# Adding the inverse transform's results by accumulating DMAs, with the second angle table built from sixteen direct slots

## The chip, the cores and the metric

The kernel runs on one core of a Trainium2 chip. The metric is the device time of one execution in microseconds, taken as the median of the runs shown. The engines are named as in the profile: PE (TensorE), ACT (ScalarE), DVE (VectorE), POOL (GpSimd) and SP (SyncE, which here only issues DMAs).

## The reference, cut to what matters

The input `x` has 2048 rows of 512 channels in bfloat16. The output is a gated mix of two branches:

```python
x = A_u                                            # (1, 2048, 512)
g = sigmoid((x * gate_w).sum(-1, keepdims=True))
a = _A_ref(x, ...)                                 # a long convolution per channel
b = _B_ref(x, ...)                                 # x plus a small FFN on the two rows that a router picks
return g * a + (1 - g) * b
```

Branch A convolves each channel `d` with a kernel of 2048 taps, which is a sum over 128 complex states, and adds a skip term:

```python
dt = exp(log_dt)[:, None]
logdA = dt * (A_re + 1j * A_im)                    # (512, 128)
P = exp(logdA[:, :, None] * l[None, None, :])      # l = 0..2047, rounded to bfloat16
K = einsum("dn,dnl,dn->dl", C, P, dt * B).real     # (512, 2048)
y = irfft(rfft(u, 2L) * rfft(K, 2L))[:L] + u * Dskip
```

## The kernel before

**What it computes in which order.** The 512 channels are worked in two halves of 256 (`h`, 0 and 1); the 2048 rows in two blocks of 1024 (`blk`). The stages are:

- `exps1` and `exps2` (L534 to L542): ACT computes magnitudes exp(t * dt * A_re) for both halves at once. `exps2` writes one copy for half 0 (`EB[0]`) and one to a staging place (`ST`), which a DMA parks in DRAM (L876) and another reads back for half 1 (L892).
- `routing` (L613): transposes, gate and router values, the FFN of the two picked rows.
- `tab1(h)` (L562): the first angle table, 32 slots of 256 values per part; `trig` (L543) supplies sines and cosines in groups of up to four slots: angle multiplies (L408), a Sin on ACT, a quarter-turn shift on DVE (L557), a second Sin.
- `tab2(h)` (L587): the second angle table `TQ[h]`, 21 slots of 256 values, real and imaginary, multiplied by the weights `w` (`WW`). Nine slots are computed directly and multiplied by `w` in one complex product; twelve more follow by two complex products of the first ones with two base factors (`BN`). `cmul` (L572) is one complex product of six DVE instructions.
- `forward` (L713): the transform of the input by matmuls (L731, L733).
- `xupd` (L864): `U` becomes (1 - g) times branch B's output.
- `kgen(h)` (L743): multiplies the two tables on PE into the kernel's taps by lag (L751), evacuates them to `KA[h]`, and regroups them by selection matmuls (L765 to L771) into `KC[h]`.
- `kspec(h)` (L775): the taps' spectrum by matmuls with the constant `KP` (L787).
- `products(h, qd, blks)` (L793): spectrum times spectrum on DVE, in quarters.
- `inverse(h)` (L826): matmuls back to rows (L841). For half 0, and for half 1's block 1, ACT writes g times the result to `YA` (L850), and a DVE addition of 128x1024 adds four rows of it to `U` (L854). For half 1's block 0 a DVE instruction does both from PSUM (L859). Then SP issues the stores, one for every two row tiles (L862).

**What sets the order.** Every operation is recorded with what it reads and writes (`Prog.op`); places in SBUF overlap, and a place can only be written when its last readers are done. `Prog.schedule` (L107) then plans the order of each engine by estimated costs: the operation that can start earliest goes first, and among equals the one with the longest estimated path to the end plus its priority:

```python
key = (st, -o.bl - o.prio)
```

Operations with a `tset` go by phases: all of phase 0 (the exponentials) is placed before any of phase 1 (Sin, Tanh, Silu). The engines run their queues strictly in the planned order. `EV` and `SCL` may go to ACT or DVE, as the planner finds earlier.

**Places that matter here.** `TQ[0]`, `ST`, `EB[1]` and `KA[1]` share one region; `TQ[1]`, `EB[0]` and `KA[0]` another. So the parked magnitudes can only be read back when `kgen(0)` has read all of `TQ[0]`, and `tab2(1)` can only write `TQ[1]` when half 0's selection has read `KA[0]`. `KP` lies where `TP[0]` was. `YA` has two parts by `t2`, which each block of rows reuses.

Of the kernel before, what the change touches and what calls it, by code (L numbers as in the profile page):

```python
# [9 lines left out]
BF = mybir.dt.bfloat16  # L10
# [48 lines left out]
class Prog:  # L59
# [47 lines left out]
    def schedule(self):  # L107
# [15 lines left out]
        dma_free = {SP: 0.0, ACT: 0.0}  # L123
# [135 lines left out]
T2 = [0, 1, 2, 3, 258, 256, 512, 768, 4, 5, 6, 7, 262, 260, 516, 772, 1024, 1280, 1536, 1792, 2048]  # L259
T2BASE = [(0, 4), (13, 17), (8,)]  # L260
NJ = len(T2)
ANG2 = [124 + t for t in T2[:8]] + [1148, 1024, 4]
MAG2 = [None] + T2[1:8] + [1024, 4]
NM = len(MAG2)
# [64 lines left out]
def bass_gated_mix__ssm_conv_s4__moe_arch_mod__prompt_kernel(nc, A_u, A_A_re, A_A_im, A_B_re, A_B_im, A_C_re, A_C_im, A_log_dt, A_Dskip,  # L329
# [24 lines left out]
    with ExitStack() as es:  # L354
# [85 lines left out]
        EB = [B("eb%d" % i, o, NM * 512) for i, o in enumerate((oG, oE))]  # L440
        ST = B("st", oE, NM * 512)
        PK = Buf(P, "park", AR[:, :], "dram", 0, 4, BF)
        park = nc.dram_tensor("park", (128, NM * 256), BF).ap()
        QA = [B("qa%d" % i, o + NM * 512, 9 * KB) for i, o in enumerate((oG, oE))]
        BN = [(B("bni%d" % i, o + 14 * KB, KB), B("bnr%d" % i, o + 15 * KB, KB)) for i, o in enumerate((oG, oE))]
# [91 lines left out]
        def exps2(ts):  # L537
            for b in (EB[0], ST):
                P.op(POOL, lambda h, b=b: h.memset(b(0, 128, 0, (4 * NM, 64), (1, 4)), 1.0), [], [(b, ("e", 0))], cost=0.4)
            for i, m in enumerate(MAG2):  # L540
                if i:
                    AC(two(EB[0], ST, i * 4, 4 * NM), AL(0, 128, 0, (HC, 2), (4, 64), (1, 4)), ACTF.Exp, [AL], [(EB[0], ("e", i)), (ST, ("e", i))], scale=float(m), tset=ts)  # L542
        def trig(h, angs, ts, neg):  # L543
# [5 lines left out]
            na_ = len(angs)  # L549
            ks = [(a, i) for i in range(na_)]  # L550
            lo = bass.AP(ah.tensor, ah.offset, [[ah.ap[0][0], 128], [2 * HC, na_], [8, 64], [2, 4]])
            n = na_ * HC
            def so(k):
                return s(0, 128, k * n, (4, na_), (4 * na_, 64), (1, 4))
# [17 lines left out]
        def cmul(h, outs, a, b, rda, rdb, wr):  # L572
            t = QA[h]
            o3 = outs(0).ap[1:]
            def q(i):
                d, st = [], 1
                for s_, c_ in reversed(o3):
                    d.insert(0, (st, c_))
                    st *= c_
                return t(0, 128, i * 9 * HC, *d)  # L580
            TT(q(0), a(0), b(0), MUL, rda + rdb, [(t, 0)])
            TT(q(1), a(1), b(0), MUL, rda + rdb, [(t, 1)])
            TT(outs(1), a(1), b(1), MUL, rda + rdb, wr(1))
            TT(outs(0), a(0), b(1), MUL, rda + rdb, wr(0))
            TT(outs(1), outs(1), q(0), SUB, [(t, 0)], wr(1))
            TT(outs(0), outs(0), q(1), ADD, [(t, 1)], wr(0))
        def tab2(h, ts):  # L587
            (qi, qr), (bi, br), eb = TQ[h], BN[h], EB[h]
            tq = lambda p: (qi, qr)[p]
            TW = 4 * NJ  # L590
            for g in range(3):
                s = trig(h, ANG2[4 * g:4 * g + 4], ts[g // 2], False)
                nn = len(ANG2[4 * g:4 * g + 4])
                for b_, kk, o_s, sk in ((qi, "s", 0, "s"), (qr, "c", 2 * nn * HC, "c")):
                    if g < 2:
                        TT(b_(0, 128, 16 * g, (TW, 64), (1, 16)), eb(0, 128, 16 * g, (4 * NM, 64), (1, 16)), s(0, 128, o_s, (16, 64), (1, 16)), MUL,
                           [(eb, ("e", 4 * g + i)) for i in range(4)] + [(s, sk)], [(b_, ("a", g))])
                    else:
                        bb = bi if b_ is qi else br
                        TT(b_(0, 128, 32, (TW, 64), (1, 4)), eb(0, 128, 32, (4 * NM, 64), (1, 4)), s(0, 128, o_s, (12, 64), (1, 4)), MUL,  # L600
                           [(eb, ("e", 8)), (s, sk)], [(b_, ("a", 2))])
                        TT(bb(0, 128, 0, (8, 64), (1, 8)), eb(0, 128, 32, (4 * NM, 64), (1, 8)), s(0, 128, o_s + 4, (12, 64), (1, 8)), MUL,
                           [(eb, ("e", 8)), (eb, ("e", 9)), (s, sk)], [bb])
            ka = lambda p: [(tq(p), ("a", g)) for g in range(3)]
            ks = ka(0) + ka(1)
            sl = lambda p, j, c: tq(p)(0, 128, 4 * j, (TW, 64), (4, c), (1, 4))
            cmul(h, lambda p: sl(p, 0, 9), lambda p: sl(p, 0, 9), lambda p: WW(0, 128, (1 - p) * D + h * HC, (4, 64), (0, 9), (1, 4)), ks, [WW], ka)
            bn = lambda p, j, c: (bi, br)[p](0, 128, 4 * j, (8, 64), (0, c), (1, 4))
            cmul(h, lambda p: sl(p, 13, 8), lambda p: sl(p, 0, 8), lambda p: bn(p, 1, 8), ks, [bi, br], lambda p: [(tq(p), "n")])
            cmul(h, lambda p: sl(p, 9, 4), lambda p: sl(p, 5, 4), lambda p: bn(p, 0, 4), ks, [bi, br], lambda p: [(tq(p), "f")])  # L610
# [132 lines left out]
        def kgen(h):  # L743
# [12 lines left out]
            for bk in range(3):  # L756
                pb = misc()
                def sel(hh, bk=bk, pb=pb):
                    last = None
                    base = T2BASE[bk]  # L760
                    njg = len(base)
# [192 lines left out]
```

## Time and profile before

| what | value |
|---|---|
| median of 3 runs | 193.92 us (193.47 to 194.07) |
| the profiled execution's own time | 193.47 us |
| its span, first to last instruction | 191.7 us |
| PE busy | 160.6 us (84%), mean granted clock 0.972 |
| DVE busy | 163.5 us (85%), 240 instructions |
| ACT busy | 130.4 us (68%), 214 instructions |
| POOL busy | 3.9 us (2%), 9 instructions |
| moved by DMA | 22.39 MB, mean 117 GB/s |

The profile is of one execution. "Busy" is the time in which an engine had an instruction under way; the span has stages with different limits, so the shares say little by themselves. A line number names the line that recorded the operation, which is often a helper: L389 is every DVE instruction on two tensors, L400 and L404 are ACT's activations and evacuations, L408 the angle multiplies, L393 instructions with a constant.

### The profile page before, as it was taken

How to read it: one execution, taken by the hardware profiler on the slowest of the kernel's cores; microseconds unless marked ns; L12 is line 12 of the kernel's file. 1: busy time of each engine (PE TensorE's matmuls, PEld its weight loads, DVE VectorE, ACT ScalarE, POOL GpSimd, SP SyncE). 2: the span in 40 equal slices, each digit the busy share in tenths (PEclk: the TensorE clock that was granted, in tenths of full speed). 3: DMA queues.
4: the chain of work that ended last, by engine and by line, in shares of the span. 5: the costliest groups of instructions: out<-in, count | busy, mean ns of one | idle time of the engine just before them, and what ended most of it. 6: DMA issues, size and time to landing. Idle time of an engine off the chain costs nothing.

```text
span 191.7 us, 3562 instructions
## 1 busy us (share of the span) xinstructions
PE 160.6 (84%) x1490; PEld 105.7 (55%) x1490; DVE 163.5 (85%) x240; ACT 130.4 (68%) x214; POOL 3.9 (2%) x9
## 2 busy tenths in 40 slices
PE   0066499999999999999998798996899999659691
PEld 0065444666344444565563166785688888437580
DVE  0658745899999999996717999999999999999983
ACT  3679999999989995499959963697345562232400
POOL 8000000000000000000000000000000000000000
PEclk9999669999999999999999999999999999978999
DMA  5999999309401202200099200000920001012133
GB/s 94 257 289 359 294 404 405 100 9 329 104 14 45 55 4 51 55 3 0 15 364 419 108 2 3 0 3 0 359 84 0 3 0 55 3 55 65 45 109 109
DMA packets 22097, 22.39 MB, mean 117 GB/s; under 512 B 13121, under 2 KB 19394, under 8 KB 21698
## 3 DMA queue, kind: packets, MB, share of 16 engines
q1 hardware_dynamic: 20738, 21.84, 35.8%
q10 hardware_dynamic: 1344, 0.33, 1.5%
q8 instruction: 11, 0.18, 0.4%
q14 instruction: 4, 0.03, 0.0%
HBM read 18.63 MB, written 2.75 MB: 112 GB/s over the span
## 4 chain that ended last, share of the span: by engine, by line
PE 46%; DVE 40%; ACT 4%; DMA 4%; issue 2%; SPq 1%; DVEq 0%
DVE AR L389 38%; PE ps L731 30%; DMA AR<-in_A_u_dram 4%; PE ps L751 3%; PE ps L841 2%; ACT AR L400 2%; ACT AR L404 2%; PE ps L733 2%; PE ps L706 2%; DVE AR L396 2%; PE ps L765 2%; PE ps L620 1%; PE ps L695 1%; SPq L484 1%; PE ps L632 1%
## 5 line engine op out<-in xcount | busy, mean ns | idle before, releaser
L389 DVE TENSOR_TENSOR AR<-AR 128x1024 bf16<-128x1024 bf16 (+7 forms) x148 | 130.4, 939 | 11.4 <-DMA AR<-in_A_A_re_dram 6.2
L404 ACT ACTIVATE AR<-ps 128x1024 bf16<-128x1024 f32 (+5 forms) x58 | 45.2, 818 | 27.0 <-PE ps L787 14.5
L731 PE MATMUL ps<-AR 128*128 128x512 bf16 x256 | 60.5, 387 | 0.0
L400 ACT ACTIVATE AR<-AR 128x512 bf16<-128x512 f32 (+4 forms) x73 | 50.5, 757 | 3.4 <-DVE AR L389 2.2
L731 PEld LDWEIGHTS ps<-AR 128*128 128x128 bf16 x256 | 24.8, 99 | 28.9 <-issue 2.3
L841 PE MATMUL ps<-AR 128*128 128x256 bf16 x256 | 30.9, 281 | 6.0 <-DVE AR L389 4.4
L841 PEld LDWEIGHTS ps<-AR 128*128 128x128 bf16 x256 | 25.3, 101 | 11.1 <-DVE AR L389 5.8
L400 ACT ACTIVATE AR<-ps,AR 128x256 bf16<-128x256 f32 (+1 forms) x40 | 19.9, 566 | 15.6 <-PE ps L841 10.2
L787 PE MATMUL ps<-AR 128*128 128x256 bf16 x224 | 26.2, 273 | 2.5 <-ACT AR L404 2.5
L787 PEld LDWEIGHTS ps<-AR 128*128 128x128 bf16 x224 | 21.3, 98 | 7.2 <-ACT AR L404 4.6
L408 ACT ACTIVATE AR<-AR 128x256 int32<-128x256 f32 (+1 forms) x41 | 17.2, 488 | 0.0
L620 PE MATMUL ps<-AR 128*128 128x128 bf16 x64 | 6.7, 289 | 11.9 <-DMA AR<-in_A_u_dram 11.0
L393 DVE TENSOR_SCALAR AR<-AR 128x1024 int32<-128x1024 int32 (+5 forms) x22 | 11.5, 529 | 1.8 <-ACT AR L400 1.5
L620 PEld LDWEIGHTS ps<-AR 128*128 128x128 bf16 x64 | 5.7, 133 | 12.7 <-DMA AR<-in_A_u_dram 11.0
L751 PE MATMUL ps<-AR 128*128 128x84 bf16 x256 | 11.7, 200 | 1.1 <-ACT AR L404 1.1
L751 PEld LDWEIGHTS ps<-AR 128*128 128x128 bf16 x256 | 10.8, 97 | 3.1 <-ACT AR L404 1.5
L869 PE MATMUL ps<-AR 128*128 128x512 bf16 x16 | 6.2, 386 | 1.7 <-ACT AR L400 1.4
L404 DVE CAST AR<-ps 128x1024 bf16<-128x1024 f32 (+1 forms) x6 | 6.8, 1125 | 0.5 <-PE ps L733 0.5
L408 DVE TENSOR_SCALAR AR<-AR 128x256 int32<-128x256 f32 (+1 forms) x21 | 5.6, 306 | 1.6 <-ACT AR L400 1.5
L765 PE MATMUL ps<-AR 128*32 128x128 bf16 (+1 forms) x96 | 6.4, 383 | 0.5 <-ACT AR L404 0.5
L404 DVE COPY AR<-ps 128x1024 bf16<-128x1024 bf16 (+1 forms) x6 | 4.1, 688 | 3.0 <-PE ps L620 2.8
L733 PE MATMUL ps<-AR 128*128 128x512 bf16 x16 | 6.1, 379 | 0.0
(37 smaller groups left out, 57.6 us busy)
## 6 DMA issues: line engine op xcount, KB each, us to landing
AR<-c_ksp SPq DMA_DIRECT2D x1, 3584.0 KB, 14.4
AR<-in_A_u_dram SPq DMA_DIRECT2D x2, 1024.0 KB, 8.7
AR<-c_fwd SPq DMA_DIRECT2D x1, 2048.0 KB, 7.9
AR<-c_fwdn SPq DMA_DIRECT2D x8, 256.0 KB, 4.3
AR<-c_inv SPq DMA_DIRECT2D x1, 2048.0 KB, 9.0
out_dram<-AR SPq DMA_DIRECT2D x16, 128.0 KB, 2.2
AR<-in_B_w_gate_dram SPq DMA_DIRECT2D x1, 1792.0 KB, 11.2
AR<-in_B_w_up_dram SPq DMA_DIRECT2D x2, 896.0 KB, 11.7
```

Source lines behind the costliest of these rows:

```text
L389: return P.op(DVE, lambda h: h.tensor_tensor(out=o, in0=a, in1=b, op=op), rd, wr, cost=tt_cost(o, a, b), **k)
L393: return P.op(DVE, lambda h: h.tensor_scalar(out=o, in0=a, scalar1=s1, scalar2=None, op0=op0), rd, wr, cost=c, **k)
L400: return P.op(ACT, lambda h: h.activation(out=o, in_=a, func=func, scale=scale, bias=bias), rd, wr, cost=0.185 + nel(o) * 0.833e-3 + (0.09 ...
L404: return P.op((ACT, DVE), (lambda h: h.activation(out=o, in_=a, func=ACTF.Copy), lambda h: h.tensor_copy(o, a)), rd, wr, cost=(0.185 + n * ...
L408: return P.op((ACT, DVE), (lambda h: h.activation(out=o, in_=a, func=ACTF.Copy, scale=c), lambda h: h.tensor_scalar(out=o, in0=a, scalar1= ...
L620: last = h.transpose(bb(0, 128, db * 256 + t_ * 128, (1, 128)), U(0, 128, (2 * q + t_) * D + db * 128, (1, 128)), IDN(0, (1, 128)))
L731: last = h.matmul(o, w, U(0, 128, (blk * 8 + st * 2 + par) * D, (1, D)), start=(par + st == 0), stop=(par * 4 + st == 7 and blk == 0))
L733: last = h.matmul(o, CB(0, 128, 640 if part == 0 else 512, (1, 128)), X(0, 128, (1 - part) * 2048 + (pm * 4 + ft) * 256, (8192, 2), (1, 25 ...
L751: last = hh.matmul(pb(0, 128, (g - b0) * 84, (1, 84)), TP[h][1 - part](0, 128, g * 128, (1, 128)), TQ[h][1 - part](0, 128, g * 84, (1, 84) ...
L765: last = hh.matmul(pb(32 * g, 32, c4, (256, njg), (4, 64)), lw, KA[h](0, 128, c4 + 4 * (base[0] + g), (16, njg), (84, 64)), start=True, st ...
L787: last = hh.matmul(pb(0, 128, n * 256, (1, 256)), KP(0, 128, u * 2048 + tau * 128, (1, 128)), KC[h](0, 128, jg * 256, (1, 256)), start=(k ...
L841: last = hh.matmul(pb(0, 128, e * 256, (1, 256)), G(0, 128, ((par * 2 + part) * 4 + ft) * 512 + (2 * t2 + e) * 128, (1, 128)), X(0, 128, h ...
```

## The change

Two things change together.

**The second table.** The list of slots `T2` is reordered. Sixteen magnitudes and angles are computed directly per half (`MAG2`, `ANG2`): eight that become slots 0 to 7, and eight multiples of 256 that become factors (`BS`). `trig` always takes four slots, so `tab2` has four groups. Groups 0 and 1 are each multiplied by `w` by a complex product of 1024 values; four more complex products (`far`, 4, 2, 2 and 5 slots) make slots 8 to 20. `cmul` uses three scratch parts where it used two and writes into its outputs only sums and differences. The parked copy and its two DMAs grow from 655,360 to 1,048,576 bytes; the read back stands behind the load of `KP` and has no priority of its own. The two POOL memsets of the exponentials' first slot go; that slot is an exponential too.

**The additions.** The DVE additions into `U` in `inverse` become DMAs issued by POOL that read `YA` and accumulate into `U`, 262,144 bytes each.

```diff
@@ -120,7 +120,7 @@
...
-        dma_free = {SP: 0.0, ACT: 0.0}
+        dma_free = {SP: 0.0, ACT: 0.0, POOL: 0.0}
@@ -256,12 +256,10 @@
 BLK, NBLK, HF, HC = 1024, 2, 2, 256
 T1 = [8 * k for k in range(16)] + [8 * (31 - k) for k in range(16)]
 ANG1 = [124 - 8 * s for s in range(16)]
-T2 = [0, 1, 2, 3, 258, 256, 512, 768, 4, 5, 6, 7, 262, 260, 516, 772, 1024, 1280, 1536, 1792, 2048]
-T2BASE = [(0, 4), (13, 17), (8,)]
+T2 = list(range(8)) + [256, 258, 260, 262, 512, 516, 768, 772, 1024, 1280, 1536, 1792, 2048]
 NJ = len(T2)
-ANG2 = [124 + t for t in T2[:8]] + [1148, 1024, 4]
-MAG2 = [None] + T2[1:8] + [1024, 4]
-NM = len(MAG2)
+ANG2 = [124 + b for b in range(8)] + [256 * a for a in range(1, 9)]
+MAG2 = list(range(8)) + [256 * a for a in range(1, 9)]
 KUSE = [(0, 0), (0, 1), (0, 2), (0, 3), (0, 4), (1, 4), (1, 5)]
 
 
@@ -437,12 +435,13 @@
         XT = B("xt", oD, 16 * KB)
         WG = B("wg", oF, 14 * KB); WD = B("wd", oF, 14 * KB)
         WU = [B("wu%d" % i, oB + (8 + 16 * i) * KB, 7 * KB) for i in range(2)]
-        EB = [B("eb%d" % i, o, NM * 512) for i, o in enumerate((oG, oE))]
-        ST = B("st", oE, NM * 512)
+        BS = [(B("bsi%d" % i, o, 4 * KB), B("bsr%d" % i, o + 4 * KB, 4 * KB)) for i, o in enumerate((oG, oE))]
+        EB = [B("eb%d" % i, o, 4 * KB) for i, o in enumerate((oG, oE))]
+        ST = B("st", oE, 8 * KB)
+        B_st = [lambda p0, n, c, *d, k=k: ST(p0, n, c + 2 * KB * k, *d) for k in range(2)]
         PK = Buf(P, "park", AR[:, :], "dram", 0, 4, BF)
-        park = nc.dram_tensor("park", (128, NM * 256), BF).ap()
-        QA = [B("qa%d" % i, o + NM * 512, 9 * KB) for i, o in enumerate((oG, oE))]
-        BN = [(B("bni%d" % i, o + 14 * KB, KB), B("bnr%d" % i, o + 15 * KB, KB)) for i, o in enumerate((oG, oE))]
+        park = nc.dram_tensor("park", (128, 4 * KB), BF).ap()
+        QA = [B("qa0", oG + 8 * KB, 7680), B("qa1", oE + 8 * KB, 7680)]
         NG = [B("ng%d" % i, oG + 16 * KB + 2 * i * KB, 2 * KB) for i in range(2)]
         ARG = [B("arg%d" % i, oI + 4 * i * KB, 4 * KB, I32) for i in range(2)]
         ARH = [b.base.bitcast(I16) for b in ARG]
@@ -535,23 +534,21 @@
             for s in range(32):
                 AC(two(TP[0][1], TP[1][1], s * 4, 128), AL(0, 128, 0, (HC, 2), (4, 64), (1, 4)), ACTF.Exp, [AL], [(TP[0][1], ("e", s)), (TP[1][1], ("e", s))], scale=float(T1[s]), tset=ts)
         def exps2(ts):
-            for b in (EB[0], ST):
-                P.op(POOL, lambda h, b=b: h.memset(b(0, 128, 0, (4 * NM, 64), (1, 4)), 1.0), [], [(b, ("e", 0))], cost=0.4)
             for i, m in enumerate(MAG2):
-                if i:
-                    AC(two(EB[0], ST, i * 4, 4 * NM), AL(0, 128, 0, (HC, 2), (4, 64), (1, 4)), ACTF.Exp, [AL], [(EB[0], ("e", i)), (ST, ("e", i))], scale=float(m), tset=ts)
+                k = i // 8
+                d = (EB[0], BS[0][1])[k]
+                AC(two(d, B_st[k], (i % 8) * 4, 32), AL(0, 128, 0, (HC, 2), (4, 64), (1, 4)), ACTF.Exp, [AL], [(d, ("e", i % 8)), (ST, i)], scale=float(m), tset=ts)
...
-            na_ = len(angs)
-            ks = [(a, i) for i in range(na_)]
-            lo = bass.AP(ah.tensor, ah.offset, [[ah.ap[0][0], 128], [2 * HC, na_], [8, 64], [2, 4]])
-            n = na_ * HC
+            ks = [(a, i) for i in range(4)]
+            lo = bass.AP(ah.tensor, ah.offset, [[ah.ap[0][0], 128], [2 * HC, 4], [8, 64], [2, 4]])
+            n = 4 * HC
             def so(k):
-                return s(0, 128, k * n, (4, na_), (4 * na_, 64), (1, 4))
+                return s(0, 128, k * n, (4, 4), (16, 64), (1, 4))
@@ -569,7 +566,8 @@
...
-        def cmul(h, outs, a, b, rda, rdb, wr):
+        def cmul(h, outs, a, b, nd, rda, rdb, wr):
+
             t = QA[h]
@@ -577,37 +575,44 @@
...
-                return t(0, 128, i * 9 * HC, *d)
...
+            TT(q(0), a(1), b(1), MUL, rda + rdb, [(t, 0)])
+            TT(q(1), a(0), b(0), MUL, rda + rdb, [(t, 1)])
+            TT(q(2), a(1), b(0), MUL, rda + rdb, [(t, 2)])
+            TT(outs(1), q(0), q(1), SUB, [(t, 0), (t, 1)], wr(1))
+            TT(q(0), a(0), b(1), MUL, rda + rdb, [(t, 0)])
+            TT(outs(0), q(2), q(0), ADD, [(t, 0), (t, 2)], wr(0))
         def tab2(h, ts):
-            (qi, qr), (bi, br), eb = TQ[h], BN[h], EB[h]
+            (qi, qr), (bi, br), eb = TQ[h], BS[h], EB[h]
             tq = lambda p: (qi, qr)[p]
-            TW = 4 * NJ
-            for g in range(3):
+            n = 4 * HC
+            for g in range(4):
                 s = trig(h, ANG2[4 * g:4 * g + 4], ts[g // 2], False)
...
+                if g < 2:
+                    im, re = [b_(0, 128, 16 * g, (4 * NJ, 64), (1, 16)) for b_ in (qi, qr)]
+                    src = eb(0, 128, 16 * g, (32, 64), (1, 16))
+                    ek = [(eb, ("e", 4 * g + i)) for i in range(4)]
+                    ki, kr = (qi, ("s", g)), (qr, ("s", g))
+                else:
+                    im, re = [b_(0, 128, 16 * (g - 2), (32, 64), (1, 16)) for b_ in (bi, br)]
+                    src = re
+                    ek = [(br, ("e", 4 * (g - 2) + i)) for i in range(4)]
+                    ki, kr = (bi, ("i", g)), (br, ("r", g))
+                TT(im, src, s(0, 128, 0, (16, 64), (1, 16)), MUL, ek + [(s, "s")], [ki])
+                TT(re, src, s(0, 128, 2 * n, (16, 64), (1, 16)), MUL, ek + [(s, "c")], [kr] + (ek if g > 1 else []))
+                if g < 2:
+                    v = lambda part: tq(part)(0, 128, 16 * g, (4 * NJ, 64), (4, 4), (1, 4))
+                    w = lambda part: WW(0, 128, (1 - part) * D + h * HC, (4, 64), (0, 4), (1, 4))
+                    cmul(h, v, v, w, n, [ki, kr], [WW], lambda p: [(ki, kr)[p]])
+            sk = [(b, ("s", g)) for b in (qi, qr) for g in range(2)]
+            b2, b3 = [(bi, ("i", 2)), (br, ("r", 2))], [(bi, ("i", 3)), (br, ("r", 3))]
+            def far(j, cnt, ss, a0, sa, rdb):
+                cmul(h, lambda p: tq(p)(0, 128, 4 * j, (4 * NJ, 64), (4, cnt), (1, 4)), lambda p: tq(p)(0, 128, 0, (4 * NJ, 64), (4 * ss, cnt), (1, 4)),
+                     lambda p: (bi, br)[p](0, 128, 4 * a0, (32, 64), (4 * sa, cnt), (1, 4)), cnt * HC, sk, rdb, lambda p: [(tq(p), ("f", j))])
+            far(8, 4, 2, 0, 0, b2)
+            far(12, 2, 4, 1, 0, b2)
+            far(14, 2, 4, 2, 0, b2)
+            far(16, 5, 0, 3, 1, b2 + b3)
 
 
         def routing():
@@ -757,18 +762,17 @@
...
-                    base = T2BASE[bk]
-                    njg = len(base)
+                    njg = 2 if bk < 2 else 1
                     for g in range(4):
                         for c4 in range(4):
                             lw = CB(0, 128, c4, (4, 32))
-                            last = hh.matmul(pb(32 * g, 32, c4, (256, njg), (4, 64)), lw, KA[h](0, 128, c4 + 4 * (base[0] + g), (16, njg), (84, 64)),
+                            last = hh.matmul(pb(32 * g, 32, c4, (256, njg), (4, 64)), lw, KA[h](0, 128, c4 + 4 * (8 * bk + g), (16, njg), (84, 64)),
                                              start=True, stop=(bk + g > 0), tile_position=(0, 32 * g))
                             if bk + g == 0:
                                 last = hh.matmul(pb(0, 32, c4, (4, 64)), CB(0, 128, 0, (1, 32)), DSK(0, 128, h * HC + c4, (4, 64)), start=False, stop=True, tile_position=(0, 0))
                     if bk == 2:
                         for c4 in range(4):
-                            last = hh.matmul(pb(0, 128, 256 + c4, (4, 64)), CB(0, 128, c4, (4, 128)), KA[h](0, 128, c4 + 48, (84, 64)), start=True, stop=True)
+                            last = hh.matmul(pb(0, 128, 256 + c4, (4, 64)), CB(0, 128, c4, (4, 128)), KA[h](0, 128, c4 + 80, (84, 64)), start=True, stop=True)
                     return last
                 P.op(PE, sel, [KA[h], CB, DSK], [pb.buf], cost=(24 if bk == 0 else 20) * 0.06)
                 EV(KC[h](0, 128, bk * 512, (1, 512)), pb(0, 128, 0, (1, 512)), [pb.buf], [(KC[h], bk)])
@@ -851,7 +855,7 @@
...
-                                    TT(u, u, YA(0, 128, t2 * 1024, (HC, 4), (1, HC)), ADD, [(YA, (p_, t2, e)) for p_ in range(2) for e in range(2)] + [(U, ("x", tb)) for tb in tbs], [(U, ("o", tb, h)) for tb in tbs])
+                                    P.op(POOL, lambda g, u=u, t2=t2: g.dma_start(u, YA(0, 128, t2 * 1024, (HC, 4), (1, HC)), accum_op=ADD), [(YA, (p_, t2, e)) for p_ in range(2) for e in range(2)] + [(U, ("x", tb)) for tb in tbs], [(U, ("o", tb, h)) for tb in tbs], cost=1.0, nbytes=262144, dma=True)
@@ -873,7 +877,7 @@
 
         exps1(0)
         exps2(0)
-        DMA([(bass.AP(park.tensor, 0, [[NM * 256, 128], [1, NM * 256]]), ST(0, 128, 0, (1, NM * 256)))], [ST], [PK], 655360)
+        DMA([(bass.AP(park.tensor, 0, [[4 * KB, 128], [1, 4 * KB]]), ST(0, 128, 0, (1, 4 * KB)))], [ST], [PK], 1048576)
@@ -889,8 +893,9 @@
         P.boost = 60.0
         kgen(0)
         P.boost = 0.0
-        DMA([(EB[1](0, 128, 0, (1, NM * 256)), bass.AP(park.tensor, 0, [[NM * 256, 128], [1, NM * 256]]))], [PK], [(EB[1], ("e", i)) for i in range(NM)], 655360, prio=1e5)
         DMA([(KP(0, 128, 0, (1, 7 * 2048)), kp_c[:, :])], [], [KP], 3670016)
+        DMA([(B("eb1b", oE, 8 * KB)(0, 128, 0, (1, 4 * KB)), bass.AP(park.tensor, 0, [[4 * KB, 128], [1, 4 * KB]]))], [PK],
+            [(EB[1], ("e", i)) for i in range(8)] + [(BS[1][1], ("e", i)) for i in range(8)], 1048576)
         tab2(1, (1, 1))
         kspec(0)
         kgen(1)
```

More of the change, by code (lines that the diff above doesn't have):

```diff
@@ L579, in q @@
                     st *= c_
-                return t(0, 128, i * 9 * HC, *d)
[L581 to L586, printed above, removed]
+                return t(0, 128, i * 5 * HC, *d)
+            TT(q(0), a(1), b(1), MUL, rda + rdb, [(t, 0)])
@@ L591, in tab2 @@
-            for g in range(3):
+            n = 4 * HC
+            for g in range(4):
                 s = trig(h, ANG2[4 * g:4 * g + 4], ts[g // 2], False)
[L593 to L609, printed above, removed]
@@ L610, in tab2 @@
-            cmul(h, lambda p: sl(p, 9, 4), lambda p: sl(p, 5, 4), lambda p: bn(p, 0, 4), ks, [bi, br], lambda p: [(tq(p), "f")])
+                if g < 2:
[8 more added lines that the diff above has]
+                    ki, kr = (bi, ("i", g)), (br, ("r", g))
```

## The prediction

> **What bounds the kernel now.** I read the busy tenths first, then busy time by stage, then the chain that ended last in order of time, then groups by form and the DMA issues. The tenths of 40 slices (4.8 us each), from the page:
>
> ```profile
> PE   0066499999999999999998798996899999659691
> DVE  0658745899999999996717999999999999999983
> ACT  3679999999989995499959963697345562232400
> ```
>
> No engine bounds the whole span. ACT is full first, then PE and DVE together, then DVE alone. The cut by stage (columns: length, then each engine's busy us and instruction count, clock, DMA share, GB/s) says where:
>
> ```profile
> 0.00:34.00 34.00, 18.93 (x170) 12.29 (x171) 18.82 (x47) 27.59 (x48) 3.87 (x9) 0.90 1.02 299
> 34.00:80.00 46.00, 46.00 (x383) 23.29 (x382) 45.20 (x72) 40.55 (x65) 0.00 (x0) 1.00 0.27 73
> 80.00:100.20 20.20, 20.20 (x239) 12.53 (x237) 13.33 (x18) 16.88 (x28) 0.00 (x0) 1.00 0.27 87
> 100.20:123.90 23.70, 20.86 (x137) 12.29 (x135) 22.53 (x27) 17.04 (x25) 0.00 (x0) 1.00 0.28 118
> 123.90:180.10 56.20, 47.29 (x507) 39.19 (x504) 55.89 (x65) 28.39 (x50) 0.00 (x0) 0.97 0.17 57
> ```
>
> (a) To 34 us ACT runs the exponentials. (b) 34 to 80: trigonometry, first tables of both halves and second table of half 0; DVE lacks 0.8 of 46 us, PE runs the forward transform beside it. (c) 80 to 100.2: PE is full with `kgen(0)` between forward groups, and DVE idles 7 us. (d) From 100.2 DVE is full: second table of half 1 until 123.9, then products. The chain confirms the ends of this DVE run (start, us, what):
>
> ```profile
> 79.99 0.90 PE ps L751 x24
> ...
> 94.21 0.30 PE ps L751 x8
> ...
> 99.61 0.59 PE ps L771 x4
> ...
> 154.89 22.21 DVE AR L389 x27
> ...
> 180.15 4.67 PE ps L841 x40
> ```
>
> L751 is `kgen`, L771 the last selection matmul, L841 the inverse. At the end PE, not DVE, carries the chain: from 180.15 one run of 64 inverse matmuls follows the first pair of the last products.
>
> **The prices**, from groups by form (mean ns):
>
> ```profile
> L389 DVE TENSOR_TENSOR AR<-AR 128x2048 bf16<-128x2048 bf16 x60 | 70.7, 1216 | 0.3
> L389 DVE TENSOR_TENSOR AR<-AR 128x1024 bf16<-128x1024 bf16 x58 | 36.9, 682 | 4.3 <-PE ps L771 4.2
> L400 ACT ACTIVATE AR<-AR 128x1024 bf16<-128x1024 int16 x24 | 24.5, 1052 | 1.1 <-DVE AR L393 0.6 <-DVE AR L389 0.4
> L400 ACT ACTIVATE AR<-AR 128x512 bf16<-128x512 f32 x41 | 21.8, 619 | 1.8 <-DVE AR L389 1.8
> ```
>
> Queued instructions overlap, so I pay the distance between starts. In the DVE timeline a 1024-wide instruction starts at 48.22 and the next at 48.82: 0.60. The two means differ by 0.534 for 1024 more elements, 0.52 ns each; so 256 wide is 0.20, 512 0.33, 1280 0.73, 2048 1.14, 2304 1.27. An instruction that needs the result just before it waits longer: in the chain 2304-wide ones start at 108.02, 109.42 and 110.81, 1.39 apart, so 0.12 more. On ACT, 24 exponentials take 12.57 us in the timeline: (12.57 - 0.62) / 23 = 0.52 each.
>
> **1. Exponentials.** 16 in place of 9 (`MAG2`), all in the phase that has to end before the first Sin. ACT has no gap between 20.29 and its table load at 32.87, so 7 x 0.52 = +3.6 us for every Sin, and DVE's stage (b) hangs on those. DVE has some 1 us to draw forward (idle pieces before 35.4, conversions of forward groups). Taken: +2.7 to +3.6. The two POOL memsets that go (0.31 each) are hidden.
>
> **2. Second table, each half.** Before: 8 direct products (4 of 1024, 2 of 256, 2 of 512: 3.5 us) and three complex products of six instructions (2304, 2048, 1024: 18.1). After: 8 x 0.60 = 4.8, and six complex products, 18 x 0.60 + 12 x 0.33 + 6 x 0.73 = 19.1. Both sets multiply 6 x 5376 elements; only the number of instructions differs, 44 for 26. Angle shifts at L557 go from 1024, 1024, 768 to four of 1024 (+0.7), five more angle multiplies of 256 (0.2 on DVE or 0.31 on ACT), and ACT Sins from 5.3 to 8 x 0.95 = 7.6. The new `cmul` also reuses its scratch at once, so up to three of its six instructions follow directly what they wait for: 18 x 0.12 = 2.2 at most; other work fills some.
> Half 0: +1.3 +1.0 +0.7 +0.5, about +3.5 us on a full DVE; first-table work of half 1 fills the waits.
> Half 1: g0 and g1 trigonometry lies in the idle of (c). On the path: direct 4.8, complex 19.1, two shifts 1.2, waits 1.5 (0 to 2.2): 26.6, against 23.7 now (100.23 to 123.90, with 1.0 idle for Sin that early complex products now cover). **+3.0**, bounds +1.4 to +4.7, the upper with that 1.0 of idle back.
>
> **3. When the half-1 table can start.** By 1 and 2 `kgen(0)` begins 6.5 us later, at about 86.5. PE isn't idle meanwhile: seven forward groups of 1.95 us remain at 80, it does 3.4 of them. From 86.5 each pair of `kgen` batches costs 2.85 us while a forward group is left to put between (the chain's spacing), afterwards about 1.4 (the pairs of `kgen(1)` at 128 to 132 us: 1.3 to 1.8). 3.6 x 2.85 + 1.7 x 1.4 = 12.7, end 99.2 at worst, 98.5 taken, against 94.5: +4. This hardly depends on the 6.5: each us more there moves the end by a quarter. The selection, 3.7 us, then ends about 102.9. But the parked exponentials come back only when `kgen(0)` has released their place:
>
> ```profile
> AR<-c_ksp SPq DMA_DIRECT2D x1, 3584.0 KB, 14.4
> park<-AR SPq DMA_DIRECT2D x1, 640.0 KB, 12.8
> AR<-park SPq DMA_DIRECT2D x1, 640.0 KB, 5.0
> ```
>
> The reload was issued at 94.55 and landed at 99.58, just inside the selection. It grows to 1024 KB. The constants behind it (issued 94.93, landed 109.3) took 9.7 us for 3584 KB after it, 370 KB per us, so 384 KB more is +1.0: 6.0. Issued at 98.6 it lands at 104.6, behind the selection, and becomes what DVE waits for: start 104.6 for 100.2. **+4.4**, bounds +2.5 (`kgen` ends 2 later) to +7. The store to park grows too, at 24 to 40 us beside full DMA slices; its reader of the place starts at 48.8, 11 us after it landed at 37.4.
> The queue order decides here. The reload now has no priority and stands behind the constants in the program; the planner takes the longer remaining path. With the planner's own costs I get 61 for the reload (24 serial table instructions, +1.3 for its size) and 57 for the constants, so the reload stays first.
>
> **4. The additions.** Six of 1024, 0.60 each, at 159.5, 169.3, 171.1, 175.2, 180.6 and 182.4. The first three stand in front of an instruction that would otherwise wait 0.12 for its predecessor: 0.48 each. The fourth is worth 0.60. The last two come after 180.1, when PE already runs its 7.5 us of inverse: nothing. **-2.0**, bounds 0 (other fillers) to -3.6.
> Each becomes a 256 KB DMA from the POOL queue, 512 runs of 512 bytes, SBUF to SBUF. No POOL DMA is in this trace. Nearest rows: a 128 KB output store lands in 2.2 us, a 256 KB constant in 4.3, the park store in 12.8; I take 4.5 from the second, the same size. POOL has no other work after 5 us, so only another such DMA queues there. Waiting behind: `YA`'s next writer on ACT, and the stores on SP. Half 0's first two would land by about 163.5 in today's times, as ACT wants the places at 162.4 and 164.2: no cost, and ACT's 5.0 us wait for the second addition at 170.0 goes, off the path. The last is issued at 179.3; two stores of 0.65 must go ahead of the first final one at 187.1, so it has 6.6 us: hidden at 4.5.
> The Trainium skill, "DMA: Bandwidth & Descriptors", section on the anatomy of a GpSimd DMA, gives about 2.0 us plus bytes over 436 GB/s: an estimate of 2.6, which would leave the sum as it is. "SBUF — State Buffer", section "Who interferes with whom", speaks against the change: GpSimd cannot write descriptors while DVE runs a two-port mode instruction. DVE's stage here holds tensor_tensor alone, which the page counts as taking only the read side; no run here shows either.
>
> **Sum.** +4.4 +3.0 -2.0 = +5.4. The profiled execution took 193.47 us, span 191.7 and 1.8 around it; the median of three runs is 193.92, so +0.45. 193.47 + 5.4 + 0.45 = 199.3. The three spreads, added as squares, give 196.4 to 203.1 for this case.
>
> **Rivals.**
> *The accumulating DMAs bind the tail* (0.10). Point: landing over 6.6 us. Price: landing minus 6.6; at 12.8, the slowest row, +6.2: 205.5. For it: SP issues in order, and the final stores stand behind. Against: the 256 KB row.
> *The constants go ahead of the reload* (0.06). It then lands 9.7 us later, +9.7: 209. For it: program order and the lost priority; against: the path lengths.
> *Faster* (0.06). The half-0 growth is absorbed by moving first-table work of half 1 out of 61 to 80 us, so that `kgen(0)` still begins by 80. Then the start moves 0.4 (reload 6.0 from 94.55), the table costs its +1.4, and all additions count -3.6: -1.8, 192.1. Against: DVE has 0.8 us of idle in that stage, and Sins come 3.6 later.
> *Nothing to measure* (0.04): the same with the additions at -2.0, 193.7. A measurement here tells about 0.3% from no change.
> The forecast keeps 0.74. Range 196 to 205, a little outside that below and half-way into the tail case above: it leaves out the constants-first case, the two small ones and the far end of the tail case. Slower 0.90, same 0.04, faster 0.06.
>
> **What would show it.** 48 exponentials in the 128x512 group and the table load near 36.5; first L751 at 85 to 88; reload issued near 98.6 and landing 6 later, then DVE full from about 104.6; six POOL DMAs of 256 KB landing in 3 to 6.6 us; the last inverse run of 64 matmuls unchanged. Wrong if the first L751 stays at 80, if DVE's start waits for the selection and not for the reload, or if stores on SP wait for POOL's DMAs after the inverse is done.

## The result, and the profile after

The changed kernel takes 200.3 us (median of 4 runs, 200.22 to 201.41) against 194.0 us (4 runs, 193.47 to 194.25): a ratio of 1.034, interval 1.030 to 1.038. The forecast was 199.3, range 196 to 205. The profiled execution took 200.23 us with a span of 198.4, so its span is 6.7 us longer than that of the kernel before; 1.8 us lie around it in both.

The busy tenths, 40 slices of 4.96 us now, with the row of PE's granted clock:

```profile
PE   0075599999999999999995599931988999999980
DVE  0659636599999999999678999999999999899960
ACT  3679999989999999799999976530653536542500
PEclk9998569999999999999999579995599999999996
```

ACT's longer exponential phase can't be told from its row, which is full on both sides of the table load. What can be told stands on the right: PE, which dips to 6, 5 and 6 among its last slices in before, stays at 8 or 9 from the 29th slice to the one before the last. The cut by stage, with the borders where the same events lie now (length, then busy us and instructions of PE, weight loads, DVE, ACT and POOL, clock, DMA share, GB/s):

```profile
36.64:80.00 43.36, 43.36 (x369) 22.03 (x367) 42.25 (x79) 41.86 (x67) 0.00 (x0) 1.00 0.25 69
80.00:103.72 23.72, 23.72 (x243) 13.65 (x245) 20.39 (x30) 21.80 (x36) 0.00 (x0) 1.00 0.22 75
103.72:138.09 34.37, 21.98 (x157) 13.28 (x154) 33.58 (x56) 21.36 (x30) 0.00 (x0) 0.84 0.22 94
138.09:188.47 50.38, 48.35 (x516) 42.50 (x517) 48.89 (x57) 25.51 (x46) 7.47 (x6) 0.94 0.39 85
188.47:198.40 9.93, 4.14 (x38) 3.46 (x36) 3.50 (x8) 0.00 (x0) 0.38 (x1) 0.85 0.82 154
```

The second table of half 1 lies in 103.72 to 138.09; the DVE timeline shows 8.0 us of half 0's products placed among it. The stage after the table is shorter than before by those 8.0 and 2.0 more. The last row is the one that the forecast left unchanged: from DVE's last product to the end it is 9.93 us, and was 7.40 (184.30 to 191.70). Two pieces make the 2.5: from the last product to the last sum it is 5.06 us (193.53) and was 4.04 (188.34), from there to the end 4.87 and was 3.36. The chain in order of time shows who took it over (start, us, what):

```profile
88.13 0.91 PE ps L756 x24
...
98.49 0.30 PE ps L756 x8
...
120.42 17.75 DVE AR L387 x28
138.22 6.14 PE ps L756 x84
...
171.65 18.35 PE ps L845 x168
190.03 3.10 DVE AR L394 x7
```

L756 is `kgen`, L845 the inverse, L387 every DVE instruction on two tensors, L394 the last sums from PSUM. Before, the chain ended with 25.2 us of DVE products (from 154.89 to 180.10), 4.67 us of inverse and the last sums. Now it leaves DVE at the end of half 1's table (138.17), goes on over PE and ACT's evacuations, and stays on PE alone from 155.32 to the last sums at 190.03. The waits of PE, from the first matmul of `kspec(1)` to the last of the inverse, first before, then after (who waited for whom, us in all, times, longest):

```profile
PE ps L841 <- DVE AR L389: 4.4, 4, 1.7
PE ps L841 <- ACT AR L400: 1.6, 1, 1.6
PE ps L787 <- ACT AR L404: 0.9, 2, 0.7
```

```profile
PE ps L791 <- ACT AR L402: 0.9, 2, 0.7
```

Before, the inverse waited 4.4 us for DVE's products and 1.6 us for ACT. After, it never waits; the 0.9 us that is left lies at the start of `kspec(1)`. From there on the amount of PE's work alone says when the inverse is done.

Two groups and three DMA rows answer to the forecast's prices. Groups (busy us, mean ns, idle before it):

```profile
L398 ACT ACTIVATE AR<-AR 128x512 bf16<-128x512 f32 x48 | 25.5, 624 | 1.8 <-DVE AR L387 1.8
L858 POOL DMA_DIRECT2D AR<-AR x6 | 7.8, 1396 | 177.1 <-ACT AR L398 177.1
```

DMA issues (KB each, us from issue to landing):

```profile
AR<-AR POOLq DMA_DIRECT2D x6, 256.0 KB, 4.4
park<-AR SPq DMA_DIRECT2D x1, 1024.0 KB, 13.6
AR<-park SPq DMA_DIRECT2D x1, 1024.0 KB, 4.8
```

### The profile page after: what moved, and what is told of

It reads as the page before. It is cut to its first block, busy times and chain, and to the rows that moved or that the text cites. A ratio compares the mean times of both kernels' runs of the same rounds, so it can differ in the third digit from the quotient of the medians.

```text
span 198.4 us, 3626 instructions
## 1 busy us (share of the span) xinstructions
PE 162.6 (82%) x1490; PEld 108.1 (54%) x1490; DVE 168.1 (85%) x275; ACT 140.6 (71%) x232; POOL 11.2 (6%) x13
## 4 chain that ended last, share of the span: by engine, by line
PE 70%; DVE 11%; ACT 10%; DMA 4%; SPq 1%; issue 1%; DVEq 0%
PE ps L736 29%; PE ps L845 13%; DVE AR L387 9%; PE ps L791 7%; PE ps L756 6%; ACT AR L398 5%; ACT AR L402 4%; DMA AR<-in_A_u_dram 4%; PE ps L769 3%; PE ps L738 2%; PE ps L873 2%; PE ps L711 2%; DVE AR L394 2%; PE ps L625 1%; PE ps L700 1%; PE ps L874 1%
## 5 line engine op out<-in xcount | busy, mean ns | idle before, releaser
L387 DVE TENSOR_TENSOR AR<-AR 128x1024 bf16<-128x1024 bf16 (+7 forms) x178 | 132.5, 801 | 8.9 <-DMA AR<-in_A_A_re_dram 6.4
L402 ACT ACTIVATE AR<-ps 128x1024 bf16<-128x1024 f32 (+4 forms) x56 | 43.9, 810 | 30.0 <-PE ps L791 15.5
L398 ACT ACTIVATE AR<-AR 128x512 bf16<-128x512 f32 (+4 forms) x84 | 59.5, 772 | 4.8 <-DVE AR L391 2.1
L736 PE MATMUL ps<-AR 128*128 128x512 bf16 x256 | 60.8, 388 | 0.0
L736 PEld LDWEIGHTS ps<-AR 128*128 128x128 bf16 x256 | 25.3, 100 | 30.2 <-issue 2.6
L845 PE MATMUL ps<-AR 128*128 128x256 bf16 x256 | 28.6, 273 | 0.0
L791 PE MATMUL ps<-AR 128*128 128x256 bf16 x224 | 26.0, 273 | 1.7 <-ACT AR L402 1.7
L845 PEld LDWEIGHTS ps<-AR 128*128 128x128 bf16 x256 | 25.0, 98 | 2.9
L791 PEld LDWEIGHTS ps<-AR 128*128 128x128 bf16 x224 | 21.5, 98 | 6.0 <-ACT AR L402 3.1
L406 ACT ACTIVATE AR<-AR 128x256 int32<-128x256 f32 (+1 forms) x50 | 21.1, 483 | 0.1
L756 PE MATMUL ps<-AR 128*128 128x84 bf16 x256 | 14.2, 225 | 8.0 <-DVE AR L387 7.6
L756 PEld LDWEIGHTS ps<-AR 128*128 128x128 bf16 x256 | 13.2, 113 | 10.7 <-DVE AR L387 7.9
L858 POOL DMA_DIRECT2D AR<-AR x6 | 7.8, 1396 | 177.1 <-ACT AR L398 177.1
L391 DVE TENSOR_SCALAR AR<-AR 128x1024 int32<-128x1024 int32 (+4 forms) x24 | 13.2, 551 | 0.3
L625 PEld LDWEIGHTS ps<-AR 128*128 128x128 bf16 x64 | 5.4, 128 | 13.5 <-DMA AR<-in_A_u_dram 11.2
L873 PE MATMUL ps<-AR 128*128 128x512 bf16 x16 | 7.5, 468 | 4.2 <-ACT AR L398 4.2
L874 PE MATMUL ps<-AR 128*128 128x512 bf16 x16 | 7.5, 468 | 0.0
```

What stands on the lines that cost most here:

```text
L387: return P.op(DVE, lambda h: h.tensor_tensor(out=o, in0=a, in1=b, op=op), rd, wr, cost=tt_cost(o, a, b), **k)
L391: return P.op(DVE, lambda h: h.tensor_scalar(out=o, in0=a, scalar1=s1, scalar2=None, op0=op0), rd, wr, cost=c, **k)
L398: return P.op(ACT, lambda h: h.activation(out=o, in_=a, func=func, scale=scale, bias=bias), rd, wr, cost=0.185 + nel(o) * 0.833e-3 + (0.09 ...
L402: return P.op((ACT, DVE), (lambda h: h.activation(out=o, in_=a, func=ACTF.Copy), lambda h: h.tensor_copy(o, a)), rd, wr, cost=(0.185 + n * ...
L406: return P.op((ACT, DVE), (lambda h: h.activation(out=o, in_=a, func=ACTF.Copy, scale=c), lambda h: h.tensor_scalar(out=o, in0=a, scalar1= ...
L625: last = h.transpose(bb(0, 128, db * 256 + t_ * 128, (1, 128)), U(0, 128, (2 * q + t_) * D + db * 128, (1, 128)), IDN(0, (1, 128)))
```

## The experiments

The theories after this comparison: the table alone makes the loss, and the additions' gain is handed back in the tail. Three things could hand it back: the order of PE's work there (`kspec(1)` runs interleaved with the inverse of half 0), half 0's products that the planner placed among half 1's table, and the stores on SP behind POOL's last DMAs. Ratios are against the kernel before, measured beside each group of runs (medians 193.52, 193.85 and 193.92 us), with their 95% intervals; in this section a difference of whole times given with a sign is worked out from the ratio.

**The two parts apart.** The changed kernel with the six DVE additions back:

```diff
-P.op(POOL, lambda g, u=u, t2=t2: g.dma_start(u, YA(...), accum_op=ADD), ..., dma=True)
+TT(u, u, YA(...), ADD, ...)
```

> The new table with the six VectorE additions put back, and no POOL DMA. Theory T (the table is the loss, the additions are a small gain that the tail gives back): in the changed kernel PE carries the end without a gap from 151.85 us, and the stores wait 1.6 us behind the POOL DMAs, so taking the DMAs away returns that 1.6 and the additions (2.0 on VectorE) go partly under PE: 199.5, between 198.7 and 200.8. Rival A (the additions were on the path to the end and their removal gained its 2.0): 202.3. Rival B (the POOL DMAs are the main loss, through the tail or through VectorE): under 198.

Measured: 200.28 us, 1.035 (1.031 to 1.040), as much as the whole change. The two ends of the chain differ, though:

```profile
171.70 15.87 DVE AR L387 x20
187.61 4.67 PE ps L845 x40
192.31 3.10 DVE AR L394 x7
```

Here DVE's products bind again, as in before, and end at 191.77; with the DMAs they end at 188.47. Of these 3.3 us 0.9 stood already at the start of `kspec(1)` (152.79 for 151.85), so some 2.4 are what the DMAs take off DVE. The last sum comes 2.3 earlier with the DMAs (193.53 for 195.80), but the last store is issued only 0.7 earlier (195.76 for 196.47).

The other way round, the kernel before with the additions as DMAs: all six, then half 0's four only (the edit above reversed, in the second under `if h == 0`).

> The kernel before with all six additions made accumulating DMAs on POOL, table unchanged. Theory T: -2.0 on VectorE and up to 1.6 given back by stores that stand behind the last two DMAs: 192.0 to 193.6 for 194.0. Rival A (nothing given back): 192.0. Rival B (POOL DMAs cost time): above 194.5, with the last stores waiting for POOL's DMAs by more than 2 us.

> The kernel before with only half 0's four additions as accumulating DMAs; half 1's two stay on VectorE, where they lie behind the release of the last inverse matmuls. Theory T: the gain of those ahead of 180.1 us, 3 x 0.48 + 0.60 = 2.0, and no store at the end behind POOL: 192.0, and no slower than all six. Rival A: the two of half 1 matter as well, so this is 0.6 to 1.2 slower than all six. Rival B: above 194.

Measured: 192.17, 0.993 (0.990 to 0.996), and 192.20, 0.991 (0.987 to 0.994). Half 0's four DMAs give the whole gain. With all six DVE's last product ends at 180.68, 1.1 us earlier than with four (181.81), but the last store is issued at 187.74 against 186.62: SP waits for POOL's DMAs there.

**The exponentials.** The kernel before with seven exponentials computed twice (the copies write the same slots again):

```diff
+for i in range(1, 8):
+    AC(two(EB[0], ST, i * 4, 4 * NM), AL(...), ACTF.Exp, ..., scale=float(MAG2[i]), tset=ts)
```

> The kernel before with seven exponentials more (seven of the second table's are computed twice, same values, same place), so that only the exponential phase grows, by 3.6 us. Theory T (a later Sin phase delays the first half's second table, and the forward matmuls that PE still has absorb part): the table's first matmul moves by 2.7 to 3.6, kgen(0) ends as much later because PE is interleaving at 2.85 us per pair until forward groups run out: +2.5 to +3.6, so 196.5 to 197.6. Rival C (the phase is hidden, the planner draws work forward): 194.0 to 194.6.

Measured: 195.72, 1.014 (1.009 to 1.019), +2.65 (the medians differ by 2.2). In the profiled execution the table load moves by 2.4 (32.87 to 35.31), the first `kgen(0)` by 3.9, its last matmul by 2.8, and the end of the span by 2.0.

**The order on PE in the tail.** The changed kernel with a priority for `kspec(1)`, so that it runs ahead of half 0's inverse:

```diff
+P.boost = 40.0
 kspec(1)
+P.boost = 0.0
```

> The changed kernel with half 1's spectrum matmuls given priority over half 0's inverse matmuls. In the changed kernel PE runs from 151.85 us to 192.3 without a gap, and VectorE idles 1.1 us for spectrum matmuls that were put behind inverse matmuls. Theory T1 (the sum of PE's work behind the second table sets the end, the order does not): 200.0, within 0.5 of the changed kernel. Rival O (the order is the loss: the POOL DMAs' planned landing time lifts the inverse matmuls ahead): 198.3 to 199.2.

Measured: 201.41, 1.040 (1.035 to 1.046). The last matmul of `kspec(1)` starts at 166.71 in place of 171.38, and nothing is won: PE still has no gap, and the last inverse matmul starts at 192.91 (192.34). The order isn't the loss; the amount of work is. The time is 1.1 above the changed kernel, more than the 0.5 that T1 allowed; in the profiled execution the first `kgen(0)` already comes 0.9 later (88.83 for 87.96), so this is not shown to be a cost of the order.

**Half 0's products held back** until half 1's table is complete:

```diff
-kx = lambda blk: [xk(h, blk, ...) ...]
+kx = lambda blk: [xk(h, blk, ...) ...] + ([*TQ[1]] if h == 0 else [])
```

> The changed kernel with half 0's products held until half 1's second table is complete; in the changed kernel 8.0 us of products stand between the table's instructions. The table should end at about 131.5 us for 138.1 and PE's last stretch start 6 us earlier. Theory T2 (VectorE's sum binds as soon as PE's doesn't, and the table's unfilled waits cost it 1 to 2 us): last VectorE product about 188.8, end 199.7, between 199.0 and 200.5. Rival P (the late PE stretch is worth all of the 2.5 us that the tail grew): 197.8.

Measured: 199.23, 1.027 (1.023 to 1.032). `kspec(1)` begins at 144.44, 7.4 us earlier, and 1.1 us arrives at the end: PE now waits 5.9 us for DVE's products again, which end at 189.21. The two engines are within 1 us of each other in the changed kernel; freeing one shows the other.

**The stores.** The changed kernel with only half 1's two additions back on DVE:

```diff
+if h == 0:
     P.op(POOL, ... accum_op=ADD ...)
+else:
+    TT(u, u, YA(...), ADD, ...)
```

> The changed kernel with half 1's two additions back on VectorE; half 0's four stay accumulating DMAs on POOL. Theory T3 (the last stores stand 1.6 us behind POOL's last two DMAs on SP): 198.7, with the first of the last four stores issued right after the first VectorE result. Rival N (nothing at the end hangs on the POOL DMAs): 200.3.

Measured: 198.70, 1.025 (1.020 to 1.029), 1.6 us better than the whole change. SP's waits for tiles to store, from 180 us on, show why; the first line is the changed kernel, the fence after it this one:

```profile
SPq L409 <- DMA AR<-AR: 13.2, 4, 6.7
```

```profile
SPq L409 <- DMA AR<-AR: 5.3, 2, 4.9
SPq L409 <- DVE AR L394: 3.5, 2, 3.2
```

In the changed kernel the stores of block 1 stand in SP's queue ahead of the four final ones and wait for POOL's last two DMAs (issued 186.26 and 187.01, stores at 190.51 and 192.53). The first of the four final stores needs the fifth of the eight last sums, which ends at 192.26; the stores go out at 193.77 to 195.76. With the additions on DVE they follow the sums: the fifth ends at 192.68, and the stores go out at 192.71 to 194.61, although the sums end 0.4 later (193.95 for 193.53).

**The rival that the constants go first.** The kernel before, its reload without the priority, so that 3584 KB of constants stand ahead of it:

```diff
-DMA([(EB[1](...), park...)], [PK], ..., 655360, prio=1e5)
+DMA([(EB[1](...), park...)], [PK], ..., 655360)
```

> The kernel before without the reload's priority: by path lengths of 57 against 56 the planner puts the 3584 KB of constants ahead of the 640 KB of parked magnitudes. Nothing else changes. Theory T (the price that the prediction's rival named, 9.7 us of constants in front, less the 0.7 by which the reload now lands before the selection is done): +8.5 to +9, 202 to 203. Rival D (earlier spectrum matmuls let products fill VectorE meanwhile): under 198.

Measured: 204.0, 1.052 (1.048 to 1.057), +10.2. The reload lands 12.5 us after its issue, and DVE shows it:

```profile
DVE AR L389 <- DMA AR<-park: 11.3, 1, 11.3
```

The table then waits 3.0 us more for a Sin, which theory T did not have; it put the time at 202 to 203. The rival's price of 9.7 was near; the rival did not occur, since the reload kept its place in the changed kernel.

**What a microsecond of table is worth.** From the kernel with 198.7, first without slots 12 to 15 of half 0, then of half 1 (two complex products, 4.0 us of DVE in each case; part of the convolution's kernel is left out), and third with seven exponentials replaced by ones that POOL writes (their slots then hold wrong values). The edit of the first two:

```diff
+if h != 0:            # second kernel: h != 1
     far(12, 2, 4, 1, 0, b2)
     far(14, 2, 4, 2, 0, b2)
+else:
+    ...               # POOL writes zeros
```

> The changed table with half 1's two additions on VectorE (198.7 us in its run), less twelve instructions of 512 elements of half 0's second table: slots 12 to 15 of half 0 are set to zero by POOL instead, so part of the convolution's kernel is left out. That is 12 x 0.33 = 4.0 us of VectorE in the stage before kgen(0). Theory Q (PE still has forward groups to do, so that a later first table moves the end of kgen(0) by a third or a quarter): -1.0 to -1.6, 197.1 to 197.7. Rival F (what VectorE loses before kgen(0) goes to the end in full): -4.0, 194.7.

> The same with half 1's slots 12 to 15 set to zero by POOL and half 0's computed: 4.0 us less of VectorE in the stage between kgen(0) and kgen(1). Theory Q (this stage has nothing beside it, all of it is on the path): -3.5 to -4.5, 194.2 to 195.2. Rival H (PE's work behind the table or the reload sets the end): above 197.5.

> The same changed table (198.7 us) with the second-table magnitudes of seven factor slots set to one by POOL instead of computed, so that ACT runs 41 exponentials as before the change; the values of those slots are left wrong, the rest is computed. The Sin phase starts 3.6 us earlier. Theory Q: kgen(0) starts 3.6 earlier and ends 1.0 to 1.4 earlier, so 197.3 to 197.7; the seven exponentials cost 2.7 alone on the kernel before, but less on top of the larger table. Rival F (the two costs add): -2.7, 196.0.

Measured: half 0, 199.02, 1.028 (1.022 to 1.033), against 1.025 with the whole table: a miss, no gain at all can be told. Half 1, 194.84, 1.005 (1.002 to 1.008): 3.9 us of 4.0 arrive. Exponentials, 197.44, 1.020 (1.016 to 1.023): 1.3 us arrive of the 3.6 by which the table load moves (35.97 to 32.36).
The miss of half 0 in the traces: `kgen(0)` begins 5.4 earlier (82.97 for 88.40) and ends 1.6 earlier, DVE's first product of half 1 starts 0.9 earlier (it waits for the reload, which takes 5.6 us here for 4.8) and its second 1.6, then DVE waits 0.87 for a Sin that it now reaches too soon, and `kspec(1)` begins 0.8 earlier (151.30 for 152.09). The last inverse matmul follows 0.7 earlier (192.02 for 192.76). My slope of a quarter, which I had raised to a third for this run, holds for the end of `kgen(0)`, not for the end of the kernel.

**The best version.** Half 0's DMAs in the kernel before, with the priority for `kspec(1)`:

> The kernel before with half 0's additions as accumulating DMAs and half 1's on VectorE, and half 1's spectrum matmuls ahead of half 0's inverse matmuls. Theory (VectorE's sum sets the end, the order of PE's work does not): 191.6 to 192.4 as without the priority. Rival O (VectorE waits for spectrum matmuls behind inverse ones): 190.5 to 191.2.

Measured: 191.89, 0.991 (0.987 to 0.994), the same as without the priority. Both beat the kernel before by about 0.9% and the changed one by 4%. The DVE theory's 191.6 to 192.4 holds.

## Why the prediction was right, and where its steps were not

The side, the size and the main mechanism were right: +5.4 forecast, +6.3 measured by medians and +6.7 by the two spans. The split of the 6.7, each term beside its forecast:

| step | forecast | measured | from |
|---|---|---|---|
| start of half 1's table | +4.4 | +3.5 | DVE's first product 100.23 to 103.72 |
| its length on DVE | +3.0 | +2.7 | 23.67 to 34.37, less 8.0 of products |
| additions, DVE to its last product | -2.0 | -2.0 | 60.40 to 50.38 + 8.0 |
| from there to the end | 0 | +2.5 | 7.40 to 9.93 |

**1. Exponentials**: right. 48 in their group, the table load at 36.64 (36.5), 3.8 us later. Seven of them cost 2.65 in the kernel before and 1.3 in the changed one, where the growth of half 0 delays `kgen(0)` as well.

**2. The second table**: right for half 1, 26.4 us of its own for 26.6, though not by all its terms: of the 1.5 us of waits between dependent instructions only one of 0.1 shows in the starts on DVE, and 0.7 for the selection and 0.3 for an evacuation by ACT stand in their place. That it is on the path is shown by leaving 4.0 us of it out, which gives 3.9. Half 0's growth was right in kind and 1.5 us too small: the first L756 at 87.96 (86.5, sign 85 to 88).

**3. The start**: the end of `kgen(0)` is where the forecast had it, 98.79 for 98.5, and so was the reload's issue, 98.82 for 98.6. That is luck in part: `kgen(0)` began 1.5 later than forecast and took 10.8 us, not 12.0. PE's forward groups absorbed most of the delay, as said: 8.1 us at the beginning of `kgen(0)`, 4.3 at its end. What failed is the path to the table's start. I had let it wait for the reload, "384 KB more is +1.0: 6.0", with the selection done by 102.9. The reload landed in 4.8, at 103.6; the 5.0 of before, from which I had started, was slow for 640 KB (3.9 to 4.4 in four other runs). And the selection ended at 104.95, not 102.9, since one forward group still lies between `kgen(0)` and the selection (L765 before, L769 after). That group stands in the chain of before too, where I had passed over it; with it, 98.5 gives 104.2. First before, then after:

```profile
94.52 1.73 PE ps L731 x8
96.24 0.22 PE ps L733
96.46 0.33 PE ps L765
```

```profile
99.26 1.73 PE ps L736 x8
100.99 0.22 PE ps L738
101.20 0.33 PE ps L769
```

So the point that I had named as "wrong" came true: DVE's first product of half 1 follows a shift without a gap, just after the reload has landed, and the only wait that the profile shows there is the second product's, for the selection:

```profile
103.11 0.69 DVE L391 TENSOR_SCALAR AR<-AR 128x1024 int32<-128x1024 int32 x1
103.72 0.68 DVE L387 TENSOR_TENSOR AR<-AR 128x1024 bf16<-128x1024 bf16 x1
104.98 3.10 DVE L387 TENSOR_TENSOR AR<-AR 128x1024 bf16<-128x1024 bf16 x5 [0.58 <-PE ps L775]
```

The first product moved by 3.5 us and the second by 4.1 (100.84 to 104.98), for 4.4 forecast: the size is near, by another wait than the one priced. The queue order, on which 9.7 us hung, was right.

**4. The additions**: the -2.0 on DVE is what the trace shows, though not by the items of my list: 3.6 of additions went, 1.1 came back in idle, 0.89 of it at 171.0, where DVE waits for spectra of half 1 that stand behind inverse matmuls; most of the other 0.5 are unfilled waits (twelve starts on DVE come 0.12 us late in this stage, nine before). The price of one DMA was right, 4.4 us for 4.5; as the 4.5 came from loads of constants from DRAM, another kind of transfer, that is luck in part. As the trace shows 4.4 to 4.9 in these runs, the 2.6 that I had worked out from the Trainium skill ("DMA: Bandwidth & Descriptors", anatomy of a GpSimd DMA) is too little for an accumulating transfer inside SBUF; the measurement decides. The starvation of which its "SBUF — State Buffer" warns, in "Who interferes with whom", did not show: beside a DVE full of tensor_tensor, for which the page excludes it too, POOL was busy 1.28 to 1.42 us with each of five issues and 1.84 with the last, which began 0.75 us after the one before it. No run here has such an issue beside an idle DVE to compare with.

**The step that failed: "the last is issued at 179.3 ... so it has 6.6 us: hidden at 4.5".** Both times were those of before. The last two DMAs were issued at 186.26 and 187.01, the first final store had its sums at 192.26, 5.3 us after the second issue, and the store that waits for that second DMA went out 5.5 us after its issue, with another still to go ahead of the final ones. The landing was as priced, the slack was gone. So the tail rival, which I had made depend on a slow landing and given 0.10, occurred by another way and cost 1.6 us, shown by taking the two DMAs away (1.5 by the trace: 4.87 from the last sum to the end, for 3.36).

**The rival that was missing: PE becomes the bound of the tail.** I carried DVE's sum to the end and never added up what PE still has to do. Of my signs, "the last inverse run of 64 matmuls unchanged" failed: the chain's last run of inverse matmuls has 168. The time from the first matmul of `kspec(1)` to the start of the last inverse matmul:

| kernel | `kspec(1)` begins | last inverse matmul | between |
|---|---|---|---|
| before | 138.22 | 187.15 | 48.9 |
| the change | 151.85 | 192.34 | 40.5 |
| `kspec(1)` first | 152.41 | 192.91 | 40.5 |
| half 1's additions on DVE | 152.09 | 192.76 | 40.7 |
| less of half 0's table | 151.30 | 192.02 | 40.7 |
| fewer exponentials | 150.55 | 191.26 | 40.7 |
| products held back | 144.44 | 192.90 | 48.5 |

40.5 to 40.7 is PE's work without a gap, in whatever order. In before the stretch held 8.4 us more: 6.9 of waits and 1.5 that the waits don't explain (the granted clock was 0.97 there and 1.00 after). After, `kspec(1)` begins 13.6 us later, 8.0 of them because half 0's products went among half 1's table, the 8.4 are gone, and the other 5.2 reach the last inverse matmul. That costs 1.0 us against DVE's own sum (last inverse matmul 5.2 later, last product 4.2). Taking this away, by holding the products back, gave 1.1. Half 0's table gives little for another reason: most of its delay is absorbed before `kspec(1)` begins. And moving all six additions gives the changed kernel nothing because half 0's four give 1.6 (200.28 with all six additions on DVE, 198.70 with only half 1's two there) and half 1's two take 1.6 back through SP.

So the sum was near for partly the wrong reasons: 0.9 too much at the start, 0.3 too much for the table, and 2.5 too little at the end (1.0 of it PE, 1.5 the stores). What stays open is how much of the 6.7 belongs to half 0's growth by itself: the run that took 4.0 us of it away scattered from 197.7 to 200.2, and shows no more than that it is well below 4.

## What to carry to other kernels

When a change moves the middle of a kernel, add up for each engine what it still has to do after that point: an engine with idle time there becomes the bound once its start moves by more than that idle time (8.4 us here, against 13.6). Reordering its work behind that point then gave nothing here; an earlier start gave 1.1 us, about what lay between the two engines. A slack between an asynchronous transfer and its reader has to be worked out in the times of the changed kernel, and a transfer that stores in an in-order queue wait for is best used where other work follows, not for the last results. Try the two parts of a double change apart: here one was worth 0.9% and was hidden under one that cost 3.5%.

## What the runs showed of the hardware, not expected

- PE's granted clock was 0.84 in the mean from 103.72 to 138.09, with slices at 0.5, where PE was busy 22.0 of 34.4 us; in the same stage before it was 1.00, with PE busy 20.8 of 23.7. The runs don't show what sets it. In such a stretch, from 110.3 to 116.2, 11 matmuls of `xupd` took 607 to 634 ns, where the others before 110 took 377 to 399; the first 96 matmuls of `kgen(1)` took 6.58 us, 69 ns each, where groups of 24 took 1.06 to 1.11 us, 44 to 46 ns each, before. No cost of it can be seen: from the beginning of `kgen(1)` to that of `kspec(1)` are 13.6 us, and were 14.2.
- The read back of 1024 KB took 4.8 to 4.9 us (5.6 in one run) and that of 640 KB 3.9 to 5.0; behind 3584 KB in the same queue the 640 KB took 12.5.
- An accumulating DMA of 256 KB within SBUF landed in 4.4 to 4.9 us (medians of ten kernels) and kept POOL busy for 1.3 to 1.6 us at its issue (means); in the changed kernel the second of two issued 0.75 us apart landed after 5.5.
